# Attention over pairs of head pairs: 64x64 TensorE tiles for the last 64 keys, 32-column tiles for the denominators, and the first MLP weight tiles converted during attention and kept in DRAM

## The chip, the cores and the metric

The kernel runs on one core of a Trainium2 chip. The metric is the time of one execution in device microseconds (us); lower is better. The kernel before was timed three times: 1094.33 us is the median.

## What is computed

Three stages follow one another, all in float32 accuracy. B = 4 batches, H = 12 heads, S = 448 positions, D = 64.

```python
scores = cap * np.tanh(scale * np.matmul(q, k.transpose(0, 1, 3, 2)) / cap)
attn = np.exp(scores - np.max(scores, axis=-1, keepdims=True))
attn = attn / (np.sum(attn, axis=-1, keepdims=True) + 1e-09)
x = np.matmul(attn, v)                 # reshaped to 1792 tokens x 768
g = np.maximum(x @ w_in, 0.0) ** 2     # 768 x 2048
x = g @ w_out                          # 2048 x 768
out = ((x @ w1) * (x @ w2)) @ w3 @ w_out2
```

The weights arrive as float64 and are converted on the chip. A weight is then kept as a high and a low part (h, l) of the fast float32 format, and a product takes three matmuls: h.h, h.l, l.h.

## The kernel before

**Attention.** The 48 heads of a (batch, head) are taken as 24 pairs p. A pair has 448 keys for each of two heads, cut into four units t = 0 to 3, and the main loop counts units u = 4p + t from 0 to 95 (then 10 more steps to drain). Units 0 to 2 hold 128 keys of each of the two heads. Unit 3 holds the last 64 keys of both heads, one head in the upper, one in the lower 64 rows of the array. Scores stand keys by queries, so a unit is

- `emit_qk` (L403, two matmuls of 64 rows x 128 columns, side by side in two row halves of the array; unit 3: L405, one 128x128 matmul against a block-diagonal k that the host padded with zeros),
- `emit_tanh` and `emit_exp` on ACT (L412, L416),
- `emit_sum` on DVE (L427, for unit 3 two half-partition adds L431), which adds the exponentials up over key blocks,
- `emit_pv` (L441, two matmuls of 128 rows x 64 columns side by side in two column halves; for unit 3 the values of the other head are zeros from the host).

In the trace a matmul of q, k, v or of a sum leaves two records, a matmul of converted weights one. `emit_den` (L451) multiplies the summed exponentials with a column of ones, in two 64-column tiles; `evacuate` (L456, L460) copies results out of PSUM, and every three pairs sends the denominators through DRAM (`normalise`, L306 to L319): store, load spread over 128 partitions, reciprocal, store, load broadcast, multiply. DVE runs its instructions in the order written, so a DVE step that waits for one of these loads holds what is behind it.

**The loop** (L551 on) works on two units per even u and writes down the order of each engine: scores and tanh of u and u+1 on the even step, then products, and on the odd step pv of u-5 and u-4. Sums run four units behind.

**Side work in the loop.** `w_products` (L522 to L524) multiplies w3 with w_out2 during attention: 128 products of three matmuls of 384 columns each, in groups of 8. Their weights come in 40 pieces of 384 (or 256) columns through `w_piece` (two ACT or one POOL and one ACT instruction, five on DVE: L118, L120, L122, L136, L78). One piece may start for every 1/W_RATE = 2 units, and the w3 pieces share 7 buffers, which set how far pieces run ahead of products. `todo` at L564 spreads the products up to step W_END.

**The turn to the MLP.** When the last product is issued (step u = 88), the pool of side work is closed. Then four weight tiles of the first MLP (two of w_in, two of w_out, each in two halves) are fetched and converted by `weight_half` (8 halves on ACT and DVE), `split_x` splits the attention results of batches 0 and 1 into high and low parts, and `front(0)` (18 matmuls for each of two tiles) is issued in `ps_w`. After that the MLP loop takes `front(1)`, `back(0)` (36 matmuls), `front(2)`, `back(1)` and so on (L325 to L327); `front(2)` needs batch 2 split, `front(3)` batch 3. From there on TensorE has work to the end.

```python
W_RATE = 0.5
W_EVEN, W_END = 20, 82
...
todo = -(-products_left // max((W_END - u) // 2, 1)) if u > W_EVEN else 4
...
if w_open and u > 1 and wnext < len(wsrc) and wnext < u * W_RATE and w_may_start(wnext):
```

Of the kernel before, what the change touches and what calls it, by code (L numbers as in the profile page):

```python
# [21 lines left out]
def tile_kernel(ctx, tc, q, k, v, cap, w_in, w_out, w1, w2, w3t, wo2, out):  # L22
# [22 lines left out]
    KC = k.shape[3]  # L45
# [8 lines left out]
    GN = NP // 2  # L54
    W_RATE = 0.5
    ON_POOL = 12
    CHAINS = 2
    LAG = 2
    W_EVEN, W_END = 20, 82
# [14 lines left out]
    wp_d = dram.tile([NM, 128, DM], F32, name="wp_d")  # L74
    wc_d = dram.tile([NM, 9, 128, 2, HW], F32R, name="wc_d")
# [18 lines left out]
    def temp(dtype, pool=None):  # L94
        if pool is None:
            return cv.tile([128, S], dtype, name="cvx", bufs=6)[:, :HW]
        return pool.tile([128, HW], dtype, name="cvx", bufs=9)

    def to_f32(raw, first=ACT, pool=None, t=None):
# [8 lines left out]
        r, a = temp(I32, pool)[:, :n], temp(F32, pool)[:, :n]  # L108
# [47 lines left out]

    half_tiles = {}

    def weight_half(i, z):

        x = block()
        g = narrow(raws.pop(0), x[:, 0, :], x[:, 1, :])
        next(g)
        fetch_next()
        for _ in range(3):
            yield
            next(g, None)
        half_tiles.setdefault(i, []).append(x)
        if z == 1:
            wts[i] = [w for x in half_tiles.pop(i) for w in columns(x)]  # L170
# [98 lines left out]
    for i in range(2 * FC):  # L269
        pieces += [stream[i][:, z * HW:(z + 1) * HW] for z in range(2)]  # L270
# [29 lines left out]
    def normalise(b, n0, lag, lag2):  # L300


        rows = slice(2 * n0, 2 * (n0 + GN))
        F = 2 * GN * S // 128
        dt_ = stat.tile([128, F], F32, name="dt")
        POOL.dma_start(out=dt_, in_=den_d[b][rows].rearrange("h s -> (h s)").rearrange("(p f) -> p f", p=128))  # L306
        for _ in range(lag):
            yield
# [3 lines left out]
        for n in range(n0, n0 + GN):  # L312
            r = cv.tile([128, 2, HW], F32R, name="bs", bufs=2).bitcast(F32).rearrange("p t n -> p (t n)")[:, :S]
            for j in range(2):
                POOL.dma_start(out=r[j * D:(j + 1) * D], in_=rec_d[b][2 * n + j].partition_broadcast(D))
            for _ in range(lag2):
                yield
            a = acc[b][:, n, :]
            DVE.tensor_tensor(out=a, in0=a, in1=r, op=ALU.mult)  # L319
            normal.add((b, n))  # L320

# [40 lines left out]


    with ExitStack() as actx:
# [9 lines left out]
        NU = NPAIR * 4  # L374
        loaded, vals, units, pvs, sums, dens = {}, {}, {}, {}, {}, {}


        sel = stat.tile([128, D + GN - 1], F32, name="sel")

        def load_qk(p):  # L380
            if p < NPAIR:
                b, hp = divmod(p, NP)
                rk = ap_.tile([128, KC], F32, name="rk", bufs=2)
# [5 lines left out]
        def load_v(p):  # L389
            b, hp = divmod(p, NP)  # L390
            vals[p] = ap_.tile([128, NT, D], F32, name="rv", bufs=3)
            SP.dma_start(out=vals[p], in_=v[b, hp])

        def emit_qk(u):

            p, t = divmod(u, 4)
            rk, rq = loaded[p]
            sc = ps_s.tile([128, 2, 512], F32, name="sc")
            ks = slice(128 * t, 128 * t + 128)
            if t < 3:  # L400
                for j in range(2):
                    r = slice(j * D, (j + 1) * D)
                    PE.matmul(sc[:, j, :S], rk[r, ks], rq[r, :], start=True, stop=True, tile_position=(j * D, 0))  # L403
# [3 lines left out]
            units[u] = sc[:, :2 if t < 3 else 1, :S]  # L407

        def emit_tanh(u):
            sc = units[u]  # L410
            pt = ap_.tile([128, 2, S], F32, name="pt", bufs=7)[:, :sc.shape[1], :]
            ACT.activation(pt, sc, AF.Tanh, scale=scl)  # L412
            units[u] = pt
# [4 lines left out]
        def emit_sum(u):  # L418

            p, t = divmod(u, 4)  # L420
            if t == 0:
                return
            if t == 1:
                sums[p] = ap_.tile([128, 2, S], F32, name="sum")
            ps, x = sums[p], units[u]
            if t < 3:
                DVE.tensor_tensor(out=ps, in0=units[u - 1] if t == 1 else ps, in1=x, op=ALU.add)  # L427
            else:
                for j in range(2):
                    r = slice(j * D, (j + 1) * D)  # L430
                    DVE.tensor_tensor(out=ps[r, j, :], in0=ps[r, j, :], in1=x[r, 0, :], op=ALU.add)  # L431

        def emit_pv(u):

            p, t = divmod(u, 4)
            x = units[u]
            if t == 0:
                pvs[p] = ps_v.tile([128, 512], F32, name="pv")[:, :S]
            for j in range(2):
                w, y = (vals[p][:, 3 * j + t, :], x[:, j, :]) if t < 3 else (vals[p][:, 6 + j, :], x[:, 0, :])  # L440
                PE.matmul(pvs[p][j * D:(j + 1) * D], w, y, start=t == 0, stop=t == 3, tile_position=(0, j * D))  # L441

        def emit_den(p):

            b, hp = divmod(p, NP)
            c = hp % GN
            if c == 0:
                dens[b] = ps_d.tile([128, 512], F32, name="den")[:, :S]
            ps = sums.pop(p)
            for j in range(2):  # L450
                PE.matmul(dens[b][j * D:(j + 1) * D], sel[:, GN - 1 - c:GN - 1 - c + D], ps[:, j, :],  # L451
                          start=c == 0, stop=c == GN - 1, tile_position=(0, j * D))

        def evacuate(p):
            b, hp = divmod(p, NP)
            DVE.tensor_copy(acc[b][:, hp, :], pvs.pop(p))  # L456
            if hp % GN == GN - 1:
                n0 = hp + 1 - GN
                stg = ap_.tile([128, S], F32, name="stg", bufs=1)
                DVE.tensor_copy(stg, dens.pop(b))  # L460
                for j in range(2):
                    POOL.dma_start(out=den_d[b].rearrange("(n j) s -> n j s", j=2)[n0:n0 + GN, j, :],
# [430 lines left out]
```

## Time and profile before

| | |
|---|---|
| median of 3 runs | 1094.33 us (1094.32 to 1095.29) |
| the profiled execution | 1092.96 us, its span 1091.2 us |
| TensorE (PE) busy | 1061.9 us (97%) |
| VectorE (DVE) busy | 787.7 us (72%) |
| ScalarE (ACT) busy | 535.3 us (49%) |
| GpSimd (POOL) busy | 183.4 us (17%) |
| HBM traffic | 159 GB/s over the span |

The profile is one execution. Busy times are shares of the span; a matmul's end is modelled, so a busy TensorE can still be one that changes tiles or waits a little. The chain of waits is followed back from the last instruction. Attention takes about the first quarter of the span; the two MLPs take the rest.

### The profile page before, as it was taken

To read this page: it belongs to the slowest core of one execution; us is meant where nothing else is said; L and a number is where in the kernel's file an instruction comes from. 1 tells how busy PE (TensorE), PEld (TensorE's weight loads), DVE (VectorE), ACT (ScalarE), POOL (GpSimd) and SP (SyncE) were. 2 spreads that over 40 slices of the span, in tenths; PEclk is the share of its full clock that TensorE was granted. 3 is DMA by queue.
4 is the path that set the end of the run, shared out by engine and by line. 5 is a ranking of instruction groups with operands and counts; after the bars stand their busy time and mean duration, and the time that the engine had idled before them with its cause. 6 is when DMAs were issued, how large, how long until landed. Compare 5 with 4: busy or idle time off the path is not lost.

```text
span 1091.2 us, 14399 instructions
## 1 busy us (share of the span) xinstructions
PE 1061.9 (97%) x5088; PEld 859.8 (79%) x5088; DVE 787.7 (72%) x1494; ACT 535.3 (49%) x959; POOL 183.4 (17%) x328
## 2 busy tenths in 40 slices
PE   7999999999789999999999999999999999999998
PEld 2333557654479999999999999999989997999997
DVE  5988886556766688888888888658476679456666
ACT  7888875658667655556665555443210122210100
POOL 3221121111210011100111111002232131232110
PEclk9999999999999999999999999999999999999999
DMA  6666654325324556556565565205556466756443
GB/s 204 184 183 180 172 166 130 118 88 159 94 75 145 154 169 202 179 174 187 169 200 167 157 197 190 78 10 147 172 174 203 144 189 222 211 165 211 145 145 116
DMA packets 71383, 173.95 MB, mean 159 GB/s; under 512 B 9313, under 2 KB 18577, under 8 KB 71313
## 3 DMA queue, kind: packets, MB, share of 16 engines
q0 software_dynamic: 35456, 93.86, 27.3%
q1 hardware_dynamic: 35856, 79.18, 24.9%
q8 instruction: 40, 0.66, 0.3%
q14 instruction: 31, 0.25, 0.1%
HBM read 135.88 MB, written 37.13 MB: 159 GB/s over the span
## 4 chain that ended last, share of the span: by engine, by line
PE 82%; DVE 9%; ACT 3%; DMA 2%; issue 2%; POOL 0%; SPq 0%; DVEq 0%; POOLq 0%; ACTq 0%
PE h L326 13%; PE h L327 13%; PE h L325 13%; PE y L325 10%; PE y L326 10%; PE y L327 10%; PE pv L441 3%; PE sc L403 3%; PE h L522 2%; PE h L524 2%; PE h L523 2%; DVE sum L427 1%; PE sc L405 1%; DVE acc L764 1%; ACT pt L412 1%
## 5 line engine op out<-in xcount | busy, mean ns | idle before, releaser
L326 PE MATMUL y<-gl,wb 128*128 128x448 f32 x384 | 140.6, 366 | 1.4 <-DVE gl L78 1.4
L325 PE MATMUL y<-gh,wb 128*128 128x448 f32 x384 | 140.6, 366 | 0.0
L327 PE MATMUL y<-gh,wb 128*128 128x448 f32 x384 | 140.5, 366 | 0.0
L721 DVE TENSOR_TENSOR bt<-h,bt 128x448 f32<-128x448 f32 x96 | 59.7, 622 | 91.9 <-PE h L327 75.5
L726 ACT ACTIVATE gh<-bt 128x448 fp32r<-128x448 f32 x32 | 18.5, 579 | 205.5 <-DVE bt L724 205.5
L635 DVE TENSOR_TENSOR acc<-y,acc 128x448 f32<-128x448 f32 x168 | 98.9, 619 | 21.8 <-PE y L327 21.3
L412 ACT ACTIVATE pt<-sc,scl 128x896 f32<-128x896 f32 x96 | 84.0, 910 | 36.4 <-PE sc L403 18.9
L241 POOL DMA_DIRECT2D wc_d<-bs x72 | 38.6, 536 | 344.2 <-DVE cvx L118 150.2
L764 DVE TENSOR_TENSOR acc<-y,acc 128x448 f32<-128x448 f32 x168 | 94.1, 614 | 0.0
L416 ACT ACTIVATE pt<-pt,capt 128x896 f32<-128x896 f32 x96 | 89.9, 944 | 0.0
L441 PE MATMUL pv<-pt,rv 128*64 128x448 f32 x384 | 83.5, 556 | 2.7 <-DVE acc L456 2.7
L403 PE MATMUL sc<-rq,rk 64*128 64x448 f32 x288 | 70.6, 593 | 9.8 <-ACT pt L412 5.6
L696 POOL DMA_DIRECT2D wb<-wc_d x112 | 59.4, 544 | 113.9 <-PE h L327 91.0
L326 PEld LDWEIGHTS y<-gl,wb 128*128 128x128 f32 x384 | 72.2, 188 | 7.5 <-DVE gl L78 1.8
L325 PEld LDWEIGHTS y<-gh,wb 128*128 128x128 f32 x384 | 72.2, 188 | 6.0
L327 PEld LDWEIGHTS y<-gh,wb 128*128 128x128 f32 x384 | 72.2, 188 | 6.0
L326 PE MATMUL h<-x2l,wb 128*128 128x448 f32 x192 | 71.3, 371 | 3.1 <-DVE x2l L78 3.1
L325 PE MATMUL y<-gh,raw 128*128 128x448 f32 x192 | 71.6, 373 | 2.7 <-ACT x0h L681 0.8
L114 ACT ACTIVATE cvx<-raw 128x384 int32<-128x384 uint32 (+1 forms) x136 | 72.9, 536 | 0.0
L78 DVE TENSOR_TENSOR gl<-gr,gh 128x448 fp32r<-128x448 f32 x64 | 39.6, 619 | 44.4 <-ACT gh L358 44.4
L325 PE MATMUL h<-x0h,wb 128*128 128x448 f32 x192 | 70.5, 367 | 0.8 <-ACT gr L356 0.8
L327 PE MATMUL h<-x2h,wb 128*128 128x448 f32 x192 | 71.0, 370 | 0.0
(136 smaller groups left out, 2519.7 us busy)
## 6 DMA issues: line engine op xcount, KB each, us to landing
wb<-wc_d POOLq DMA_DIRECT2D x112, 384.0 KB, 5.9
wc_d<-bs POOLq DMA_DIRECT2D x72, 384.0 KB, 3.0
raw<-w_in SPq DMA_DIRECT2D x32, 384.0 KB, 4.0
raw<-w_out SPq DMA_DIRECT2D x32, 384.0 KB, 3.7
raw<-w SPq DMA_DIRECT2D x32, 384.0 KB, 3.6
raw<-wc_d POOLq DMA_DIRECT2D x32, 384.0 KB, 3.4
rk<-k SPq DMA_DIRECT2D x24, 256.0 KB, 3.4
raw<-w3t SPq DMA_DIRECT2D x16, 384.0 KB, 4.2
```

The lines of the kernel that those rows point to most:

```text
L114: ACT.activation(r, words[:, :, 0], AF.Copy, scale=2.0 ** -29)
L325: PE.matmul(ps, wh, xh[:, i, :], start=start and i == 0, stop=False)
L326: PE.matmul(ps, wh, xl[:, i, :], start=False, stop=False)
L327: PE.matmul(ps, wl, xh[:, i, :], start=False, stop=(i == n - 1))
L403: PE.matmul(sc[:, j, :S], rk[r, ks], rq[r, :], start=True, stop=True, tile_position=(j * D, 0))
L412: ACT.activation(pt, sc, AF.Tanh, scale=scl)
L416: ACT.activation(units[u], units[u], AF.Exp, scale=capt)
L441: PE.matmul(pvs[p][j * D:(j + 1) * D], w, y, start=t == 0, stop=t == 3, tile_position=(0, j * D))
L635: DVE.tensor_tensor(out=a, in0=y, in1=a, op=ALU.add)
L696: POOL.dma_start(out=x, in_=wc_d[s % NM, j])
L721: DVE.tensor_tensor(out=t, in0=ps[j], in1=u, op=ALU.add)
L764: DVE.tensor_tensor(out=a, in0=y, in1=a, op=ALU.add)
```

## The change

**Pairs of pairs.** Two head pairs (four heads) now make seven units of full size in place of eight: three units of the first pair, one unit with the last 64 keys of all four heads, three units of the second pair. `what(u)` gives pair and t. There are 84 units. The four-head unit takes four matmuls in 64x64 tiles for the scores (L440) and four for pv (L487), one in each quarter of the array, on diagonal places, so that the two tiles of one pair write one PSUM bank in different partitions. The zero padding of k and v is gone from the host. Sums stay as many as before: two of the four half-partition adds wait for the second pair's t = 1.

**Denominators.** `emit_den` takes two pairs at once, in four 32-column tiles (L506); groups are two pairs of pairs, then one. `normalise` waits more steps (`lags`) and loads two broadcasts ahead.

**First MLP tiles.** The eight halves of the first four tiles join the side work's list `wsrc` (now 48 pieces), one behind each w3 block, in the same 7 buffers; each is stored to `w0_d` in DRAM (two DMAs), and when the side work closes eight DMAs on POOL's queue load them back. `w_piece` may start 0.57 per unit up to u = 40 and one per unit after that. `front(0)` and now also `back(0)` come from `first_unit`, in `ps_w`; `fill` is first called when batch 0 is split. `w_store` copies a product group out of PSUM on the odd step.

```diff
+    GD = 2
+    W_RATE = 0.57, 1.0
+    W_FAST = 40
-    W_EVEN, W_END = 20, 82
+    W_EVEN, W_END = 18, 72
...
+            if kind == "w0":
+                for s, x in enumerate(parts):
+                    POOL.dma_start(out=w0_d[i, z, :, s, :], in_=x)
+                w3_done.add(wsrc[n])
...
+        def what(u):
+
+            d, x = divmod(u, 7)
+            return 2 * d + (x > LAST), x if x <= LAST else x - LAST - 1
...
-                PE.matmul(sc[:, 0, :S], rk[:, ks], rq, start=True, stop=True)
+                for z in range(2):
+                    rk, rq = loaded[p + z]
+                    for j in range(2):
+                        r, c = slice(j * D, (j + 1) * D), j ^ z
+                        PE.matmul(sc[c * D:(c + 1) * D, z, :S], rk[r, 128 * t:], rq[r, :], start=True, stop=True,
+                                  tile_position=(j * D, c * D))
...
+                pv_tile(p + 1)
+                for z in range(2):
+                    for j in range(2):
+                        r = slice((j ^ z) * D, (1 + (j ^ z)) * D)
+                        PE.matmul(pvs[p + z][j * D:(j + 1) * D], vals[p + z][r, 6, :], x[r, z, :],
+                                  start=z == 1, stop=z == 0, tile_position=((j ^ z) * D, j * D))
...
+            for z in range(2):
+                ps = sums.pop(p + z)
+                for j in range(2):
+                    r = 32 * (2 * z + j)
+                    PE.matmul(dens[b][r:r + 32], sel[:, GD - 1 - c:GD - 1 - c + 32], ps[:, j, :],
+                              start=c == 0, stop=c == n - 1, tile_position=(0, r))
...
+                lags = (6, 4, 3) if b < B - 1 else (6, 3, 1) if n == GD else (4, 3, 1)
...
-                            ready = [weight_half(i, z) for i in range(2 * FC) for z in range(2)]
-                            side.append(chain(*(split_x(b) for b in range(EARLY))))
+                            for i in range(2 * FC):
+                                halves = [block() for _ in range(2)]
+                                for z, x in enumerate(halves):
+                                    POOL.dma_start(out=x, in_=w0_d[i, z])
+                                wts[i] = [w for x in halves for w in columns(x)]
+                            side.append(splits())
```

**Order on TensorE, early in the attention, before** (sc are scores, h products, pv, den denominators; x4 counts matmuls):

```order
L403 MATMUL sc<-rq,rk 128x448 x4
L522 MATMUL h<-wb,w3h 128x384
L523 MATMUL h<-wb,w3h 128x384
L524 MATMUL h<-wb,w3l 128x384
L441 MATMUL pv<-pt,rv 64x448 x4
L403 MATMUL sc<-rq,rk 128x448 x2
L405 MATMUL sc<-rq,rk 128x448
L522 MATMUL h<-wo_388,w3h 128x384
L523 MATMUL h<-wo_388,w3h 128x384
L524 MATMUL h<-wo_388,w3l 128x384
L441 MATMUL pv<-pt,rv 64x448 x4
L451 MATMUL den<-sum,sel 64x448 x2
```

and with the change (L431 scores of full units, L440 and L487 the four-head unit, L480 pv, L506 denominators):

```order
L506 MATMUL den<-sum,sel 32x448 x4
L431 MATMUL sc<-rq,rk 128x448 x4
L589 MATMUL h<-wb,w3h 128x384
L590 MATMUL h<-wb,w3h 128x384
L591 MATMUL h<-wb,w3l 128x384
L480 MATMUL pv<-pt,rv 64x448 x2
L487 MATMUL pv<-pt,rv 64x448 x4
L431 MATMUL sc<-rq,rk 128x448 x4
L589 MATMUL h<-wo_750,w3h 128x384
L590 MATMUL h<-wo_750,w3h 128x384
L591 MATMUL h<-wo_750,w3l 128x384
L480 MATMUL pv<-pt,rv 64x448 x4
```

The rounds of scores, products and pv stay as they are; a round in seven units each has four matmuls more in its scores, its pv and its denominators, in tiles of another shape, and there are 42 rounds in place of 48.

**Order on TensorE behind the last product, before**: the products end when six units have no scores yet.

```order
L524 MATMUL h<-wo_847,w3l 128x384
L441 MATMUL pv<-pt,rv 64x448 x4
L403 MATMUL sc<-rq,rk 128x448 x2
L405 MATMUL sc<-rq,rk 128x448
L441 MATMUL pv<-pt,rv 64x448 x4
L451 MATMUL den<-sum,sel 64x448 x2
L403 MATMUL sc<-rq,rk 128x448 x4
L441 MATMUL pv<-pt,rv 64x448 x4
L403 MATMUL sc<-rq,rk 128x448 x2
L405 MATMUL sc<-rq,rk 128x448
L441 MATMUL pv<-pt,rv 64x448 x4
L451 MATMUL den<-sum,sel 64x448 x2
```

and with the change:

```order
L591 MATMUL h<-wo_831,w3l 128x384
L480 MATMUL pv<-pt,rv 64x448 x4
L506 MATMUL den<-sum,sel 32x448 x4
L487 MATMUL pv<-pt,rv 64x448 x4
L480 MATMUL pv<-pt,rv 64x448 x6
L506 MATMUL den<-sum,sel 32x448 x2
L318 MATMUL h<-x1h,wb 128x448
L506 MATMUL den<-sum,sel 32x448 x2
L318 MATMUL h<-x0h,wb 128x448
```

All scores now stand ahead of the last product, at step u = 82 of 84; behind it there are pv of six units, two groups of denominators, and the MLP. Behind these rows 35 more matmuls of `front(0)` follow, and then those of `front(1)` and `back(0)` in turns.

**Order on DVE near the end of attention, before** (conversions L118, L120, L122 and L78 wb of the first MLP tiles between sums L427, splits x0l, and the multiply of `normalise` L319):

```order
L78 TENSOR_TENSOR wb<-cvx,wb 128x384
L78 TENSOR_TENSOR x0l<-acc_66,x0h 128x448
L118 TENSOR_SCALAR cvx<-cvx 128x384
L120 SCALAR_TENSOR_TENSOR cvx<-cvx 128x384
L122 ISA cvx<-cvx 128x768
L427 TENSOR_TENSOR sum<-pt 128x896
L78 TENSOR_TENSOR x0l<-acc_66,x0h 128x448
L118 TENSOR_SCALAR cvx<-cvx 128x384
L120 SCALAR_TENSOR_TENSOR cvx<-cvx 128x384
L122 ISA cvx<-cvx 128x768
L427 TENSOR_TENSOR sum<-sum,pt 128x896
```

and with the change (L461 and L467 sums, L511 pv and L517 denominators out of PSUM, L80 splits):

```order
L517 COPY stg<-den 128x448
L80 TENSOR_TENSOR x0l<-acc_66,x0h 128x448
L461 TENSOR_TENSOR sum<-pt 128x896
L467 TENSOR_TENSOR sum<-sum,pt 64x448 x2
L80 TENSOR_TENSOR x0l<-acc_66,x0h 128x448
L511 COPY acc_69<-pv 128x448
L461 TENSOR_TENSOR sum<-sum,pt 128x896
L80 TENSOR_TENSOR x0l<-acc_66,x0h 128x448 x2
L511 COPY acc_69<-pv 128x448
L80 TENSOR_TENSOR x0l<-acc_66,x0h 128x448 x2
L517 COPY stg<-den 128x448
```

No conversion stands there any more.

## Rows read from the trace of the kernel before

**Rows 1.** The page: span, TensorE's busy time, its granted clock in 40 slices.
```profile
span 1091.2 us, 14399 instructions
PE 1061.9 (97%) x5088; PEld 859.8 (79%) x5088; DVE 787.7 (72%) x1494; ACT 535.3 (49%) x959; POOL 183.4 (17%) x328
...
PEclk9999999999999999999999999999999999999999
```

**Rows 2.** Busy time by stretch: length; PE, PEld, DVE, ACT, POOL; clock, DMA share, GB/s.
```profile
0.00:20.07 20.07, 14.07 (x45) 4.48 (x45) 8.43 (x18) 14.02 (x18) 5.75 (x9) 1.00 0.64 204
20.07:115.45 95.38, 90.46 (x397) 35.65 (x397) 86.32 (x160) 81.48 (x115) 24.71 (x33) 0.98 0.60 178
115.45:253.22 137.77, 137.77 (x677) 83.07 (x675) 85.51 (x167) 90.85 (x132) 25.79 (x48) 1.00 0.47 144
253.22:311.50 58.28, 48.12 (x209) 29.12 (x208) 45.50 (x87) 42.99 (x81) 12.42 (x23) 0.97 0.36 105
311.50:1091.20 779.70, 771.46 (x3764) 707.51 (x3764) 561.90 (x1065) 305.98 (x616) 114.71 (x216) 1.00 0.53 163
```

**Rows 3.** The same view for line L522 alone: one matmul of each product.
```profile
20.07:115.45 95.38, 10.87 (x19) 3.69 (x19) 0.98 0.60 178
115.45:253.22 137.77, 40.72 (x109) 20.49 (x109) 1.00 0.47 144
```

**Rows 4.** The chain of waits, 109 to 118 us: start, length, what.
```profile
109.65 0.95 PE sc L403 x4
110.60 0.95 PE sc L405 x2
111.55 0.17 PE h L522
...
113.12 1.65 PE pv L441 x8
114.77 0.75 PE den L451 x4
115.53 1.71 PE sc L403 x8
117.23 0.37 PE h L522
```

**Rows 5.** The timeline at 131.55 to 131.60 us: start, length, engine, line, count.
```profile
131.52 0.20 PEld L441 LDWEIGHTS pv<-pt,rv 128*64 128x64 f32 x4 [0.25 <-issue]
131.52 0.60 PE L441 MATMUL pv<-pt,rv 128*64 128x448 f32 x2
```

**Rows 6.** Waits in the first 312 us: total, times, longest.
```profile
DVE acc L319 <- DMA bs<-rec_d: 22.4, 6, 5.1
```

**Rows 7.** TensorE's timeline: three of its idle times, with what ended them.
```profile
65.90 1.29 PE L403 MATMUL sc<-rq,rk 64*128 64x448 f32 x4 [2.10 <-ACT pt L412]
...
98.37 1.72 PE L441 MATMUL pv<-pt,rv 128*64 128x448 f32 x8 [2.19 <-DVE acc L456]
...
288.61 2.41 PE L451 MATMUL den<-sum,sel 128*64 128x448 f32 x4 [2.74 <-DVE sum L431]
```

**Rows 8.** One pair of the first stage, by the view of Rows 2.
```profile
71.74:80.67 8.93, 8.93 (x43) 3.57 (x41) 8.53 (x16) 8.26 (x13) 1.75 (x4) 1.00 0.78 222
```

**Rows 9.** The chain of waits where the MLP starts.
```profile
298.88 2.40 DMA rec_d<-dt
...
302.09 3.05 DMA bs<-rec_d
...
305.23 0.62 DVE acc L319
...
312.57 0.74 PE h L326
```

**Rows 10.** The page: POOL's issue of a weight load, and its time to landing.
```profile
L696 POOL DMA_DIRECT2D wb<-wc_d x112 | 59.4, 544 | 113.9 <-PE h L327 91.0
...
wb<-wc_d POOLq DMA_DIRECT2D x112, 384.0 KB, 5.9
```

More of the change, by code (lines that the diff above doesn't have):

```diff
@@ L298, in split_x, with normalise @@
             yield
[L300 to L305, printed above, removed]
+    def normalise(b, n0, n1, lags):
+        rows = slice(2 * n0, 2 * n1)
+        dt_ = stat.tile([128, 4 * GD * S // 128], F32, name="dt")[:, :2 * (n1 - n0) * S // 128]
         POOL.dma_start(out=dt_, in_=den_d[b][rows].rearrange("h s -> (h s)").rearrange("(p f) -> p f", p=128))
-        for _ in range(lag):
+        for _ in range(lags[0]):
             yield
@@ L361, in front, with back, first_unit @@
             yield
+    def back(n, pool, name="y", some=NO // 2):
+        c, b = divmod(n, B)
+        gh, gl = gtiles[n % 2]
+        ws = [wts[4 * c + FC + m] for m in range(FC)]
+        for o in range(NO):
+            y = pool.tile([128, 512], F32, name=name)[:, :S]
+            products(y, [w[o] for w in ws], gh, gl)
+            a = acc[b][:, o, :]
+            if c == 0:
+                ACT.activation(a, y, AF.Copy)
+            else:
+                DVE.tensor_tensor(out=a, in0=y, in1=a, op=ALU.add)
+            if c == NC - 1 or o == NO - 1:
+                flush()
+            if c == NC - 1 and (b == 0 or b == 1 and o >= NO // 2):
+                xh, xl = (x[:, o, :] for x in xs[b])
+                ACT.activation(xh, a, AF.Copy)
+                late.append((xl, a, xh))
+            tick(3)
+            if (o + 1) % some == 0:
+                yield
+    def first_unit(pool):
+        yield from front(0, pool)
+        flush()
+        yield from back(0, pool, "h", 2)
     with ExitStack() as actx:
@@ L423, in emit_sum @@
             if t == 1:
[L424 to L427, printed above, removed]
-            else:
[L429 to L441, printed above, removed]
+                sums[p] = ap_.tile([128, 2, S], F32, name="sum", bufs=3)
@@ new lines, in emit_sum, with pv_tile @@
+            if t < LAST:
+                DVE.tensor_tensor(out=sums[p], in0=units[u - 1] if t == 1 else sums[p], in1=units[u], op=ALU.add)
+            z = p % 2
+            if t == LAST or z and t == 1:
+                x = units[u - z * 2]
+                for j in range(2):
+                    r = slice((j ^ z) * D, (1 + (j ^ z)) * D)
+                    DVE.tensor_tensor(out=sums[p][r, j, :], in0=sums[p][r, j, :], in1=x[r, z, :], op=ALU.add)
+        def pv_tile(p):
+            pvs[p] = ps_v.tile([128, 512], F32, name="pv")[:, :S]
@@ L500, in w_piece @@
-            g = narrow(*blocks[0], on=DVE, first=POOL if n < ON_POOL else ACT, pool=wq)
+            kind, i, z = wsrc[n]
+            raw = wraw.pop(n)
+            if kind == "wo":
+                x = block() if i < 5 else wq.tile([128, 2, HW], F32R, name=f"wo{i}{z}")
+                parts = [x[:, 0, :], x[:, 1, :]]
+            else:
+                nj = raw.shape[-1] // 128
+                tiles = [wq.tile([128, 3, 128], F32R, name=f"w3{s}", bufs=W3)[:, :nj, :] for s in "hl"]
+                parts = [x.rearrange("p a c -> p (a c)") for x in tiles]
@@ L501, in w_piece @@
+            g = narrow(raw, *parts, on=DVE, first=POOL if n < ON_POOL else ACT, pool=wq)
             next(g)
@@ L605, in tile_kernel @@
                 advance(norms)
-            while chains or ready:
-                while ready and len(chains) < CHAINS:
-                    chains.append(ready.pop(0))
-                advance(chains)
-            while fronts < FC:
-                first = first or front(0, ps_w)
-                next(first)
-                fronts += 1
+            assert not w_open
+            while side:
+                advance(side)
+            for _ in fill:
+                pass
     mp = ctx.enter_context(tc.tile_pool(name="mlp", bufs=2, reuse_waits="tile"))
@@ L870 @@
         "q": pairs(q),
-        "k": kk,
+        "k": pairs(k),
         "v": vv,
```

257 lines of the change are left out of this document (122 added, 135 removed).

## The prediction

> **What bounds the kernel now.** I read the page first, then busy time by stretch, then the chain of waits, then single idle times. TensorE is busy for 97% of the span, at the upper level of its granted clock in every slice [rows 1]. So only what TensorE does, or waits for, can change the time. The stretches [rows 2] part the span by what ends last. From 20.07 to 115.45 us (units 8 to 47, ten head pairs) DVE is busy 86.3 of 95.4 us, and TensorE 90.5. From 115.45 to 253.22 (ten more pairs, and 109 of the 128 products [rows 3]) TensorE is busy without a gap. From 253.22 to 311.5 (last eight units, first MLP matmuls) it idles for 10.2 us, and DVE (45.5) and ACT (43.0) are busy for much of it: they convert the first MLP tiles there. From 311.5 on the MLPs run: 779.70 us for 3764 matmuls, 0.207 each. That part is not touched. I call the three stretches A, B and C.
>
> **Prices on TensorE** [rows 4]. Eight score matmul records take 1.71 us, four take 0.95. So one unit is 0.76, and 0.19 is what the first matmul behind a change of tile shape loses. A product behind the scores loses the same (0.37 against 0.17 to 0.18 for the next); three such matmuls, 0.525, make a product. pv of two units is 1.65: 2 x 0.75 and a change of 0.15. The denominators behind pv, in tiles of the same shape, are 0.75 and lose nothing. A pair is two rounds: 1.71 + 0.19 + 1.65 = 3.55, and 0.95 + 0.95 + 1.65 + 0.75 = 4.30; together 7.85. Test on B: 10 x 7.85 + 109 x 0.525 + 1.9 (the last scores and the change behind them) = 137.6, where the row has 137.8.
>
> **A pair of pairs after the change.** Seven units are 3.5 rounds of 3.55, or 12.43. The four-head unit breaks the row of equal tiles once in the scores and once in pv: 2 x 0.15. The denominators of both pairs, in four 32-column tiles, are 0.75 and a change of 0.15. Sum 13.63, against 15.70: 2.07 saved, twelve times: 24.8 us of TensorE's work. The trace has no group of four 64x64 tiles. Its bounds are 0.75 us (all four at once, as two tiles are now) and 3.0 (one after the other). I take 0.75: two tiles run together in both directions, row halves in the scores and column halves in pv, at the same price, so quarters are nearest to that. The row behind it [rows 5] shows the two first matmuls of pv running, with four weight loads at their side.
>
> A change of shape might be dear only towards full tiles: the denominators of before change nothing, so these rows do not price a change among column tiles. [...]
>
> **A.** TensorE needs 10 x 6.81 + 16 x 0.525 = 76.5 us for the same ten pairs (with the change 112 products are left at unit 42). DVE does what it did: the adds stay the same in number, and 0.57 pieces x 3.5 units are two pieces a pair, as 0.5 x 4 were. So DVE bounds A: at least its busy 86.3, at most the 95.4 of now. Among what it loses now are loads of `normalise` [rows 6], behind which TensorE idles (2.10 and 2.19 us) [rows 7]. The new lags wait six and four units where three were waited for, so the loads are there. In a pair without such a wait DVE is busy 8.53 of 8.93 us [rows 8]. I take the middle, 91: **4.4 us saved** (0 to 9).
>
> **B.** From the scores of unit 42 to the last product at unit 82 there are 40 units x 1.947 + 112 x 0.525 + 1.9 = 138.6, against 137.8, for 11.4 pairs in place of ten. The pieces of the first MLP tiles lie beside it: by the price of a pair with its two pieces [rows 8], DVE has 11.4 x 8.53 = 97 us and ACT 11.4 x 8.26 = 94 to do, under 139. But the weights come later, through the same seven buffers, so I add 1.5 us of waits (0 to 7). **2.3 us lost.**
>
> **C.** Behind the last product TensorE has no scores left: pv of six units (6 x 0.75 + 0.45), two groups of denominators (2 x 0.90), then `front(0)`, `back(0)` and `front(1)`: 108 x 0.207 = 22.4. Sum 29.1. Waits: the last denominators wait for the last sum, as at 288.61 [rows 7], 2.7; `front` reuses the one buffer of `ps_w` behind ACT, 1; splits of batch 2 stand on DVE behind multiplies of the last `normalise`, whose loads take 2.40 and 3.05 [rows 9]. There 7.3 us pass between the multiply at 305.23 and TensorE's next matmul at 312.57; I take 4 of them, since the same order remains (0 to 7.3). Sum 36.8, against 58.3: **21.5 us saved** (11 to 29). What hides the conversions now gone from C was DVE and ACT; their work moved into B, under TensorE. SP's queue fetches these eight halves earlier, in the same number. POOL gets 16 stores, 8 loads and 16 more small DMAs, at 0.54 us of issue [rows 10]: 22 us, spread over stretches where it is busy 63 of 291 us [rows 2]. The eight loads issue in 4.4 us; the first lands after 5.9 [rows 10], before TensorE has done pv and denominators (6.8 + 2.7).
>
> **Sum.** -4.4 + 2.3 - 21.5 = -23.6 us, against the profiled execution of 1092.96: 1069.4. The median of the runs lies 1.4 above it: 1094.33 - 23.6, about **1071 us**. About 0.2% (2 us) is what a measurement of this kernel tells from no change.
>
> **Rivals.**
>
> 1. *Two at a time.* The four 64x64 tiles run as two and two, 1.5 us a group: 1.5 us more per pair of pairs. A hides it (76.5 + 7.5 = 84, under 91); B holds 5.7 pairs of pairs, 8.6 us; C one pv group, 0.75. Sum 9.3: **1080 us**. Against it speaks the timeline [rows 5], where the column halves share all rows and still load weights while matmuls run; for it: no row has four. [...]
>
> 2. *One at a time: slower than before.* If tiles on the four quarters wait for each other, a group takes 3.0 us, 4.5 more per pair of pairs. In A TensorE then needs 76.5 + 22.5 = 99, 8 over DVE's 91; B grows by 25.7, C by 2.3. Sum 36: **1107 us**. It turns the sign from about 2.4 us a group on, where A's slack is used up as well. Against it: the two shapes that the chain shows [rows 4] both run two at a time.
>
> 3. *Late weights.* The stored tiles come back over the same engines as SP's next fetches. C moved 105 GB/s [rows 2], and 384 KB at that rate is 3.7 us; then the fourth half lands 17 us behind the last product, where `front(0)` asks for it at about 15. The waits in B may also be the full 7. Either gives 5 to 8 us: **1077 us**.
>
> **How the numbers follow.** Forecast 0.70, rival 1 0.11, rival 3 0.12, rival 2 0.05, and 0.02 that gains and new waits cancel. The low end takes A at -9, B at +0.8 and C at -25: 1061. The high end takes rival 1 together with half of rival 3's waits: 1087. Faster by over 0.2%: 0.93; within: 0.02; slower: 0.05.
>
> **What would show it.** In the changed profile: L440 with its eight records at 0.9 us in the chain, not 1.65; L506 at 0.9 or less; DVE nearly without idle time up to unit 42, at about 111 us; no gap on TensorE from there to the last product at about 250; from there some 37 us to the first matmul on batch 2. It is wrong if the four-head records start in pairs 0.75 us apart (rival 1), if TensorE idles before L589 for weights of a product, or if it idles before L318 for the stored tiles (rival 3).

## The result, and the profile after

The changed kernel takes **1077.28 us** (median of 4 runs, 1076.24 to 1079.31), the kernel before beside it 1094.32: a ratio of 0.9846, 95% interval [0.9829, 0.9863]. So it is faster by 17.0 us, where the prediction had 23.3. The forecast of 1071 lies 6.3 us below the measured time, and the range of 1061 to 1087 holds it. The profiled execution of the change took 1076.87 us, 16.09 less than that of the kernel before.

The page of the changed kernel, as in [rows 1]:

```profile
span 1075.1 us, 14546 instructions
...
PE 1047.7 (97%) x5136; PEld 846.2 (79%) x5136; DVE 790.0 (73%) x1502; ACT 527.8 (49%) x927; POOL 204.6 (19%) x368
...
PEclk9899999999899999999999999999999999999999
```

TensorE is busy 14.2 us less, and at 97% of the span still what bounds the kernel. Its granted clock, 9 in every slice before (a 9 stands for 0.90 or more; by stretch it was 0.97 to 1.00 [rows 2], and 0.50 from 66.52 to 69.93, from 288.38 to 291.80 and from 312.28 to 315.69 us), now shows an 8 in two, at 27 to 54 and at 269 to 296 us.

Busy time by stretch (columns as in [rows 2]), cut where the work is the same as before: start of unit 8, scores of unit 42, end of the last product, first matmul on batch 2, first matmul on batch 3, end.

```profile
0.00:21.18 21.18, 14.40 (x57) 4.40 (x57) 8.64 (x18) 14.76 (x18) 6.68 (x9) 1.00 0.67 212
21.18:108.17 86.99, 80.50 (x396) 28.52 (x396) 83.03 (x157) 78.64 (x104) 23.58 (x32) 0.94 0.63 187
108.17:246.50 138.33, 138.08 (x756) 81.13 (x752) 112.40 (x221) 106.00 (x148) 41.05 (x76) 1.00 0.60 181
246.50:279.73 33.23, 29.72 (x147) 20.71 (x147) 16.74 (x31) 16.00 (x32) 16.26 (x31) 1.00 0.52 155
279.73:302.20 22.47, 19.88 (x80) 16.47 (x78) 14.87 (x30) 16.81 (x35) 2.36 (x4) 0.85 0.26 73
302.20:1075.10 772.90, 765.12 (x3709) 694.92 (x3707) 554.34 (x1049) 295.54 (x594) 114.71 (x216) 1.00 0.54 163
```

The same view of the kernel before, for the last three of these stretches:

```profile
253.22:305.76 52.54, 44.43 (x193) 26.45 (x193) 39.90 (x75) 40.65 (x76) 11.27 (x21) 0.97 0.38 110
305.76:325.63 19.87, 16.75 (x73) 14.51 (x72) 14.12 (x29) 12.90 (x27) 1.15 (x2) 0.91 0.20 58
325.63:1091.20 765.57, 758.40 (x3709) 695.68 (x3707) 553.37 (x1049) 295.43 (x594) 114.71 (x216) 1.00 0.54 165
```

Read down the lengths against each other. Unit 42 has its scores at 108.17, where unit 48 had them at 115.45: 7.3 us won (8.4 in the stretch itself, less 1.1 lost ahead of unit 8). The next stretch is 138.33 against 137.77: 0.6 lost. From the last product to batch 2, 33.23 against 52.54, and from there to batch 3, 22.47 against 19.87: 16.7 won. And then the last row, the one that the change does not touch: 772.90 against 765.57. **7.3 us lost**, with the same 3709 matmul records, the same clock of 1.00, and 6.7 of the loss are busy time of TensorE (765.12 against 758.40), not waiting. The sum, -7.3 + 0.6 - 16.7 + 7.3, is the -16.1 of the two spans.

The chain of waits in the stretch that TensorE bounds (columns as in [rows 4]):

```profile
126.30 1.65 PE pv L480 x8
127.96 0.89 PE den L506 x8
128.84 1.71 PE sc L431 x8
130.55 0.90 PE pv L480 x4
131.45 0.91 PE pv L487 x8
...
138.50 1.65 PE pv L480 x8
140.16 0.91 PE sc L440 x8
141.07 0.95 PE sc L431 x4
142.02 0.38 PE h L589
```

All eight records of a four-head group take 0.91 us, in the scores (L440) and in pv (L487), and the denominators in 32-column tiles (L506) 0.89. That is 0.75 and a change of shape of 0.15, as the sum had it. TensorE's timeline and its weight loads at one such group (columns as in [rows 5]):

```profile
161.26 0.21 PEld L440 LDWEIGHTS sc<-rq,rk 64*64 64x64 f32 x8 [0.65 <-issue]
161.27 0.98 PE L440 MATMUL sc<-rq,rk 64*64 64x448 f32 x8
```

and the same row in a narrower window, 161.2 to 161.4 us, with what had started by then:

```profile
161.27 0.61 PE L440 MATMUL sc<-rq,rk 64*64 64x448 f32 x4
```

The first four of the eight records start within 0.02 us of each other, last 0.59 us each and lie inside 0.61 us: the four tiles run side by side. All eight loads lie inside the first 0.21 us.

Where TensorE waits at the turn to the MLP (its timeline, as in [rows 7]):

```profile
253.94 0.44 PE L318 MATMUL h<-x1h,wb 128*128 128x448 f32 x1 [0.62 <-DMA wb<-w_d]
256.00 0.94 PE L506 MATMUL den<-sum,sel 128*32 128x448 f32 x4 [1.62 <-DVE sum L461]
...
285.63 0.48 PE L319 MATMUL h<-x2l,wb 128*128 128x448 f32 x1 [1.65 <-DVE x2l L80]
...
288.69 0.74 PE L319 MATMUL h<-x2l,wb 128*128 128x448 f32 x1 [0.72 <-DVE x2l L80]
289.23 0.57 PE L320 MATMUL h<-x2h,wb 128*128 128x448 f32 x1
```

The stored tiles are 0.62 us late, the last sum 1.62, low parts of batch 2 1.65 and 0.72. Matmuls behind these last two take longer: the granted clock of 288.69 to 293.50 is 0.57 (0.50 from 285.99 to 292.81), and the step from matmul to matmul at 0.50 is 0.37 us in place of 0.207 at 1.00. What DVE did ahead of them, by its timeline:

```profile
279.31 0.62 DVE L311 TENSOR_TENSOR acc<-acc,bs 128x448 f32<-128x448 f32 x1 [4.66 <-DMA bs<-rec_d]
279.85 0.62 DVE L80 TENSOR_TENSOR x2l<-acc,x2h 128x448 fp32r<-128x448 f32 x1
...
284.42 0.62 DVE L311 TENSOR_TENSOR acc<-acc,bs 128x448 f32<-128x448 f32 x1
284.96 1.15 DVE L80 TENSOR_TENSOR x2l<-acc,x2h 128x448 fp32r<-128x448 f32 x2
```

A multiply of `normalise` for batch 3 waits 4.66 us for its load, and the splits of batch 2 (L80) stand behind it and its successors, and behind conversions of the next tiles (L120 to L124, from 282.97 on).

### The profile page after: what moved, and what is told of

It is laid out like the page before. It is cut to its first block, busy times and chain, and to the rows that moved or that the text cites. A ratio compares the mean times of both kernels' runs of the same rounds, so it can differ in the third digit from the quotient of the medians.

```text
span 1075.1 us, 14546 instructions
## 1 busy us (share of the span) xinstructions
PE 1047.7 (97%) x5136; PEld 846.2 (79%) x5136; DVE 790.0 (73%) x1502; ACT 527.8 (49%) x927; POOL 204.6 (19%) x368
## 4 chain that ended last, share of the span: by engine, by line
PE 85%; DVE 11%; ACT 2%; issue 1%; DMA 1%; SPq 0%; POOL 0%; DVEq 0%; ACTq 0%
PE h L318 14%; PE h L319 14%; PE h L320 14%; PE y L318 10%; PE y L319 10%; PE y L320 10%; PE sc L431 3%; PE pv L480 3%; PE h L589 2%; DVE sum L461 2%; PE h L591 2%; PE h L590 2%; DVE sum L467 1%; DVE acc L825 1%; DVE cvt L124 1%
## 5 line engine op out<-in xcount | busy, mean ns | idle before, releaser
L318 PE MATMUL y<-gh,wb 128*128 128x448 f32 x372 | 137.0, 368 | 0.0
L319 PE MATMUL y<-gl,wb 128*128 128x448 f32 x372 | 136.9, 368 | 0.0
L320 PE MATMUL y<-gh,wb 128*128 128x448 f32 x372 | 136.1, 366 | 0.0
L787 ACT ACTIVATE gh<-bt 128x448 fp32r<-128x448 f32 x32 | 18.5, 579 | 206.7 <-DVE bt L785 206.7
L447 ACT ACTIVATE pt<-sc,scl 128x896 f32<-128x896 f32 x84 | 80.9, 1013 | 27.2 <-PE sc L431 14.4
L451 ACT ACTIVATE pt<-pt,capt 128x896 f32<-128x896 f32 x84 | 86.9, 1047 | 0.0
L431 PE MATMUL sc<-rq,rk 64*128 64x448 f32 x288 | 71.5, 608 | 12.6 <-ACT pt L447 8.4
L320 PEld LDWEIGHTS y<-gh,wb 128*128 128x128 f32 x372 | 69.9, 188 | 6.7
L318 PEld LDWEIGHTS y<-gh,wb 128*128 128x128 f32 x372 | 69.7, 187 | 7.0
L319 PEld LDWEIGHTS y<-gl,wb 128*128 128x128 f32 x372 | 69.9, 188 | 6.2
L319 PE MATMUL h<-x2l,wb 128*128 128x448 f32 x192 | 72.1, 376 | 2.6 <-DVE x2l L80 2.6
L80 DVE TENSOR_TENSOR gl<-gr,gh 128x448 fp32r<-128x448 f32 x64 | 39.6, 621 | 45.5 <-ACT gh L351 45.5
L318 PE MATMUL h<-x2h,wb 128*128 128x448 f32 x192 | 71.9, 374 | 0.0
L320 PE MATMUL h<-x2h,wb 128*128 128x448 f32 x192 | 71.8, 374 | 0.0
```

Of the source, the lines that this page charges most:

```text
L80: DVE.tensor_tensor(out=l, in0=src, in1=h.bitcast(F32), op=ALU.subtract)
L318: PE.matmul(ps, wh, xh[:, i, :], start=start and i == 0, stop=False)
L319: PE.matmul(ps, wh, xl[:, i, :], start=False, stop=False)
L320: PE.matmul(ps, wl, xh[:, i, :], start=False, stop=(i == n - 1))
L431: PE.matmul(sc[:, j, :S], rk[r, 128 * t:128 * t + 128], rq[r, :], start=True, stop=True, tile_position=(j * D, 0))
L447: ACT.activation(pt, units[u], AF.Tanh, scale=scl)
```

## Experiments

Eleven kernels were run, for three questions: what the untouched MLP stretch lost its 7.3 us to; what each part of the change is worth; and which waits are left. The expectations count time from the first matmul (3.9 to 4.2 us into the span) where they speak of the first matmul on batch 3, and end at the start of the last matmul: the 302.20 and 772.90 of the rows above are 298.3 and 767.1 there.

### What the MLP stretch lost

The changed kernel needs fewer small tiles (`sel` is 132 bytes per partition in place of 264, `dt` 112 in place of 84), and so everything allocated behind them lies 96 bytes lower (96 and not 104, which fits tiles rounded up to 32 bytes): the ring of weights `wb` begins at byte 91392 of a partition in place of 91488, and `raw`, x2, x3, gh1 and gl1 move by the same 96. x0, x1 and gh0 come from the other side and stay. The first runs moved them with unused bytes and changed no instruction.

The changed kernel, 32 bytes:

```diff
     capt = stat.tile([128, 1], F32, name="capt")
+    stat.tile([128, 8], F32, name="pad")
```

> The changed kernel with 32 unused bytes per partition ahead of the tiles of weights, so that raw, wb, x2, x3, gh1 and gl1 begin 32 bytes past a multiple of 64, as they did in the kernel before (in the changed kernel they begin on a multiple of 64); no instruction differs. In the traces at hand the same MLP work, from the first matmul on batch 3 to the end, takes 760.7 us before and 767.1 after, at a granted clock of 1.00 in both, by a median step from matmul to matmul of 203 and 206 ns. Theory 1, the place of the tiles sets the step: 203 ns here, and about 6 us less: 1071. Theory 2, the step differs by execution or by chip: no difference by this edit, 1077, and the step may be either. Theory 3, the changed order of work or its traffic costs the 6 us: 206 ns and 1077.

Measured: 1071.70 us, ratio 0.9798 [0.9781, 0.9815]. The time is what theory 1 named, 5.6 us less than the change, but the median step stayed at 206; a part of the steps became much shorter (those on the low parts of batches 0 and 1 take 199.7 and 199.4 ns in the mean, 206.3 and 206.6 in the change; by up to 0.2 ns such means hang on where the stretch is taken to begin).

The kernel before, the same line:

> The kernel before with the same 32 unused bytes, which puts raw, wb, x2, x3, gh1 and gl1 on multiples of 64; no instruction differs. Theory 1 (place of the tiles): the step becomes 206 ns, and the time about 6 us longer, 1100. Theories 2 and 3 (execution, or changed order): 1094, and by theory 3 a step of 203 ns.

Measured: 1094.88 us, ratio 1.0009 [1.0000, 1.0018]; the median step 204. So theory 1 in its first form, that a multiple of 64 makes the step 206, is wrong: this kernel has all those tiles on multiples of 64 and loses 0.9 us, not 6. What the address does is finer than that. The next run put every tile of the changed kernel where the kernel before had it: `stat.tile([128, 24], F32, name="pad")`.

> The changed kernel with 96 unused bytes per partition, which puts raw, wb, x2, x3, gh1 and gl1 exactly where the kernel before had them; x0 and x1 lie there in both already. The first four runs: from the first matmul on batch 3 to the end 767.1 us with the ring of weights wb at 91392 (the change), 766.3 at 91392 (late tiles), 762.7 at 91424, 762.0 and 761.5 at 91520 (two different kernels, with the same histogram of steps), 760.7 at 91488 (the kernel before). Theory 1, refined: the addresses as such set the step. Then 760.7 here, a median step of 203, and 1077.3 less 6.4: 1071, or a little under the run with 32 bytes. Rival: what 32 bytes gave was the move off a multiple of 64 or 128, and this gives the 762.7 of that run: 1072 to 1073. Rival: the changed work has its own price in the MLP stretch, which no address takes away: above 763.

Measured: **1071.10 us**, ratio 0.9794 [0.9780, 0.9809]. By stretch, up to the first matmul on batch 3 and from there:

```profile
0.00:302.19 302.19, 277.57 (x1428) 148.51 (x1429) 235.66 (x454) 232.25 (x333) 90.83 (x152) 0.99 0.58 174
302.19:1068.50 766.31, 758.57 (x3709) 695.00 (x3707) 553.60 (x1049) 296.02 (x594) 114.76 (x216) 1.00 0.54 165
```

The first row ends where the change's does (302.20), the second has TensorE's busy time of the kernel before: 758.57 against 758.40, for 3709 records in both. So 6.6 of the 7.3 us (772.90 to 766.31) are the place of the tiles; the 0.7 left is no more than runs of one kernel differ by. The same number from all runs, sorted by the place of the ring:

| `wb` at | x0 and x1 | kernels | TensorE busy, first matmul on batch 3 to the end (us) |
|---|---|---|---|
| 91392 | as in the change | the change; late tiles; splits first; old lags | 765.12; 764.34; 764.93; 764.98 |
| 91392 | 32 bytes lower | 32 bytes ahead of gh0 | 762.63 |
| 91392 | as in the change; x2, x3 as in the kernel before | 96 bytes in the last pool | 761.41 |
| 91424 | as in the change | 32 bytes | 760.61 |
| 91520 | as in the change | before with 32 bytes; 64-column denominators | 759.70; 759.53 |
| 91488 | as in the change | before; 96 bytes; both gains | 758.40; 758.57; 758.26 |
| 91488 | 32 bytes lower | both gains and 32 bytes | 758.81 |

Kernels that differ in their attention but have equal addresses agree within 0.8 us; the changed kernel at other addresses differs from itself by up to 6.6. Two runs asked whose address it is. The first moved x0 and x1 alone:

```diff
+                            xp.tile([128, 8], F32, name="xpad")
                             new_gtiles(xp)
```

> The changed kernel with 32 unused bytes in the pool of batches 0 and 1 alone: x0 and x1 move down by 32 bytes, everything else stays (wb at 91392, x2 and x3 too). In the trace of the change a matmul on x2 or x3 takes 206.7 ns to the next, on x0 high 203.4, on x0 low 206.3. Theory 1 (addresses): the steps on x0 and x1 change by some ns, those on x2 and x3 stay at 206 to 207; the time moves by what x0 and x1 move, within 4 us to either side of 1077. Rival (one property of the whole run, as a clock or a chip): all steps move together or none does.

Measured: 1074.09 us, ratio 0.9822 [0.9808, 0.9837]. The mean step on the low parts of x0 and x1 fell from 206.3 and 206.6 to 202.8 and 199.3 ns, those on x2 and x3 stayed at 206.4 to 206.6: theory 1 as expected. The second moved x2, x3, gh1 and gl1 alone, with `mp.tile([128, 24], F32, name="pad", bufs=1)` ahead of them:

> The changed kernel with 96 unused bytes in the last pool alone: x2, x3, gh1 and gl1 lie where the kernel before had them, the ring of weights wb, raw and the rest stay where the change put them (wb at 91392). Steps in the change: 206.6 to 206.7 ns on x2 and x3, and TensorE is busy for 765.1 us in the 3709 matmuls from the first on batch 3 to the end; at the addresses before: 203.6 to 204.2 and 758.4 to 758.6. Theory a, the address of the streamed tile sets its step: x2 and x3 fall to about 204, and the busy time by some 1000 matmuls times 2.6 ns and a share for gh1 and gl1: 761 to 763, 1073 to 1075. Theory b, the address of the weights sets it: 206 to 207 stays on x2 and x3, 765 and 1077. Theory c, their places against each other: some third value on x2 and x3, with x0 and x1 as in the change.

Measured: 1073.91 us, ratio 0.9812 [0.9795, 0.9829]. The steps on x2 and x3 became 204.9 to 205.5, neither the 206.7 of the change nor the 204 of the kernel before: theory c's third value. But the steps on the low parts of x0 and x1, which did not move, fell too, from 206.3 and 206.6 to 203.9 and 203.5. No theory had that. So the step of a matmul follows neither from the address of what it streams nor from that of its weights alone, nor, here, from the two against each other. That the place of the tiles sets it is shown; by what mechanism stays open. A rival that no run tests is that what other engines write at the same time counts: gh1 and gl1, which moved here, are written by ACT and DVE while TensorE works on other batches (in the change 14 writes each to tiles gh and gl from 302 to 400 us, of about 0.58 and 0.62 us).

### What the parts of the change are worth

Attention alone: the first four tiles are converted at the end, as before (`weight_half` put back, the eight `w0` entries taken out of the list of pieces).

```diff
-        wsrc += first
...
+                            ready = [weight_half(i, z) for i in range(2 * FC) for z in range(2)]
...
+                while ready and len(chains) < 2:
+                    chains.append(ready.pop(0))
```

> The changed attention alone: the first four MLP tiles are fetched and converted where the kernel before did it, at the end of attention, two at a time, and not stored; the rest is the changed kernel. By the prediction's terms the eight conversions lie in the third stretch again, where DVE and ACT are what ends last: 8 halves of about 2.4 us on DVE, so 12 to 20 us longer: 1089 to 1097. Rival: the attention's own shortening is what saved the third stretch, and the conversions hide beside pv and denominators: 1077 to 1081.

Measured: 1092.93 us, ratio 0.9996 [0.9983, 1.0008]. The stretches from the last product to batch 2, to batch 3 and to the end:

```profile
234.10:297.50 63.40, 48.26 (x211) 27.33 (x210) 42.09 (x78) 38.85 (x69) 14.69 (x28) 0.87 0.36 109
297.50:318.87 21.37, 17.94 (x73) 15.04 (x73) 13.98 (x28) 16.21 (x34) 1.15 (x2) 0.84 0.24 66
318.87:1090.60 771.73, 764.34 (x3709) 694.40 (x3707) 554.53 (x1049) 295.79 (x594) 114.67 (x216) 1.00 0.54 163
```

The products end 12.4 us earlier than in the change, since no tiles are converted beside them, and from there to batch 3 it takes 84.8 us in place of 55.7. So moving the conversions gains 29.1 there for 12.4 beside the products: it is worth 16.7 us. What is left, 325.63 to 318.87, is 6.8 us for the pairs of pairs, and the place of the tiles (764.34) eats it. The first theory holds. The granted clock is lower in the first of these rows as well, 0.87 where the change has 1.00, so the 16.7 holds matmuls at the lower clock besides waits.

Denominators in 64-column tiles, pair by pair:

```diff
-                    r = 32 * (2 * z + j)
-                    PE.matmul(dens[b][r:r + 32], sel[:, GD - 1 - c:GD - 1 - c + 32], ps[:, j, :],
+                    r, k = j * D, 2 * c + z
+                    PE.matmul(dens[b][r:r + D], sel[:, 3 - k:3 - k + D], ps[:, j, :],
```

> The changed kernel with denominators in tiles of 64 columns, two tiles at a time, pair by pair (rows packed by the same sums, group sizes kept). Four matmuls then take two groups of 0.75 us without a change of shape, where the trace after shows 0.89 for all eight records, change included: 0.6 us more per pair of pairs. In the stretch that TensorE bounds (from unit 42 to the last product, 5.7 pairs of pairs) that is 3.4 us, 0.6 to 1.2 in the tail, nothing earlier: 1081. [...]

Measured: 1073.73 us, ratio 0.9817 [0.9800, 0.9834]: less than the change, which the expectation misses. The chain, and the MLP stretch:

```profile
152.20 1.66 PE pv L480 x8
153.86 1.50 PE den L506 x8
```

```profile
304.82:1073.30 768.48, 759.53 (x3709) 694.83 (x3707) 553.99 (x1049) 296.05 (x594) 114.67 (x216) 1.00 0.54 164
```

The denominators take 1.50 where the change takes 0.89. From the scores of unit 42 to the last product that makes

```profile
107.41:249.37 141.96, 141.00 (x754) 82.71 (x753) 113.54 (x222) 106.87 (x149) 36.81 (x69) 1.00 0.59 178
```

141.96 us in place of 138.33: **3.6 us lost** for 3.4 expected. Unit 42 came 0.8 earlier in this run, and the tail cost nothing more (0.6 to 1.2 was expected), so batch 3 starts 2.6 later, at 304.82 in place of 302.20. But its larger `sel` moved the ring to 91520, and the MLP stretch gave back 5.6 us of TensorE's time (765.12 to 759.53). Read by the total alone, this run would have said that 32-column tiles cost time. They save 3.6 us.

`normalise` with its old lags:

```diff
-                lags = (6, 4, 3) if b < B - 1 else (6, 3, 1) if n == GD else (4, 3, 1)
+                lags = (3, 3, 3) if b < B - 1 else (6, 3, 1) if n == GD else (4, 3, 1)
```

> The changed kernel with normalise waiting three units for each of its loads in batches 0 to 2, as before, in place of six, four and three. The prediction held that the longer waits take DVE's idle time for these loads away and that this is most of what the first stretch (units 8 to 42) gains. Then DVE waits again at L294 and L311, 1 to 2 us a group in the first stretch, where DVE ends last: 1078 to 1082, with the first scores of unit 42 at 110 to 112 in place of 108.2. Rival: the loads land within three units of the shorter rounds as well, or TensorE's shorter work is what the stretch gains: 1077 and 108 to 109.

Measured: 1083.33 us, ratio 0.9904 [0.9888, 0.9921], and the scores of unit 42 at 112.72, 4.5 us later. DVE's waits in that stretch, and idle times of ACT and TensorE behind them:

```profile
DVE acc L311 <- DMA bs<-rec_d: 3.0, 1, 3.0
```

```profile
83.94 1.01 ACT L447 ACTIVATE pt<-sc,scl 128x896 f32<-128x896 f32 x1 [4.88 <-DVE sum L461]
...
85.00 1.86 PE L431 MATMUL sc<-rq,rk 64*128 64x448 f32 x4 [4.59 <-ACT pt L447]
```

In the changed kernel no wait of DVE is listed from 21 to 108 us. One wait of 3.0 us, ended at 77.56, is enough to cost 4.5: behind it the sums are late, the tanh of the next unit waits for a tile that such a sum sets free, and the scores wait for the tanh, so that TensorE idles for 4.59. The theory holds, at a price somewhat over its range. The mark itself moves by 2 us: the other runs with the new lags have the scores of unit 42 at 106.30 to 108.44, all well ahead of 112.72.

### The waits that are left

Two waits in the first stretch were taken away by no run. TensorE waits for a tanh, and ACT for a sum on DVE, as in the run before, though DVE itself waits for nothing:

```profile
46.60 1.01 ACT L447 ACTIVATE pt<-sc,scl 128x896 f32<-128x896 f32 x1 [4.66 <-DVE sum L467]
47.66 1.86 PE L431 MATMUL sc<-rq,rk 64*128 64x448 f32 x4 [3.22 <-ACT pt L447]
...
100.50 1.91 ACT L447 ACTIVATE pt<-sc,scl 128x896 f32<-128x896 f32 x2 [1.55 <-DVE sum L467]
101.56 3.29 PE L431 MATMUL sc<-rq,rk 64*128 64x448 f32 x8 [2.45 <-ACT pt L447]
```

The granted clock behind them is 0.50 (47.66 to 53.90) and 0.62 (101.56 to 106.00). In the run with 96 unused bytes ahead of the weights (the one of 1071.10 us) the same two waits stand, 3.17 and 2.48 us, but the clock of the stretch is 1.00, and it takes 85.49 us in place of 86.99:

```profile
21.50:106.99 85.49, 76.55 (x397) 26.98 (x397) 81.48 (x154) 77.08 (x101) 23.77 (x31) 1.00 0.62 185
```

Batch 2 split ahead of the multiplies of `normalise` and of the conversions:

```diff
+                for _ in range(4 if n == 1 else 0):
+                    next(xsplit, None)
                 if n > 0:
                     advance(norms)
-                for _ in range(2):
+                for _ in range(0 if n == 1 else 2):
                     next(xsplit, None)
```

> The changed kernel, where DVE and ACT split batch 2 ahead of the last multiplies of normalise and of the conversions of the next tiles (four steps a quarter in place of two, before the multiplies); addresses as in the change. In the trace of the change TensorE waits 1.65 and 0.72 us for low parts of batch 2 behind those multiplies, and then runs 16 matmuls at 0.374 in place of 0.207, 2.7 us. Theory (the prediction's fourth wait in the third stretch: batch 2 stands on DVE behind normalise): both waits and most of the slow matmuls go, 3 to 5 us less: 1072 to 1074. Rival: the wait moves on to batch 3, whose multiplies come later now, or to ACT, which makes the high parts: 1076 to 1078.

Measured: **1071.86 us**, ratio 0.9801 [0.9786, 0.9816], at the addresses of the change. From the first matmul on batch 2 to that on batch 3:

```profile
279.99:297.36 17.37, 16.72 (x79) 14.41 (x78) 12.99 (x26) 14.33 (x32) 2.07 (x4) 1.00 0.35 106
```

17.37 us in place of 22.47, and the granted clock 1.00 in place of 0.85. The two waits were 2.4 us; the other 2.7 are the slow matmuls behind them, which went with them. Nothing of it was given back at batch 3.

Both gains together:

> The changed kernel with both edits that gained alone: batch 2 split first (first matmul on batch 3 at 293.4 us in place of 298.3) and 96 unused bytes (760.6 us from there to the end in place of 767.1). They touch different stretches, so the gains add: 1077.3 less 4.9 and 6.5, 1066; first matmul on batch 3 at 293 to 294, and 760.6 from there. Rival: the faster matmuls of the MLP stretch meet a later wait (ACT or DVE behind the earlier splits) and give 1 to 3 us back: 1067 to 1069.

Measured: **1066.40 us**, ratio 0.9738 [0.9725, 0.9751], 0.7 us short of the sum of the two. Batch 3 starts at 298.57 (294.5 by the count of the expectation, just outside its 293 to 294), 1.2 us later than with the first edit alone, and TensorE is busy for 758.26 us from there. With x0 and x1 lowered besides:

> The same with x0 and x1 32 bytes lower besides, which took 2.0 to 7 ns from the steps on their low parts with the ring at 91392 (206.3 to 202.8, 206.6 to 199.3). If each operand's own address sets the step, x0 and x1 fall again by as much, some 750 matmuls by 1 to 2 ns in the mean: 1 us less than the run with both edits, 1065. If what counts is an address beside the ring's, the effect at this place of the ring is another, and may be a loss: 1064 to 1068, with the steps on x2 and x3 unchanged at 203.7 to 204.2 either way.

Measured: 1065.63 us, ratio 0.9737 [0.9724, 0.9750], no difference from the run before. The steps on the low parts of x0 and x1 became 205.0 (from 204.7 and 203.7), and those on x2 and x3, which had not moved, 202.5 to 203.3 (from 203.6 to 204.0). The expectation that these stay was wrong, as in the run on the last pool. There is a pattern, though: the steps on x0 to x3 are now, within 0.5 ns, those of the two kernels with the ring at 91520 (x0 high 205.3 against 205.4 in both, x2 high 202.9 against 202.8 and 202.9). Against those, the ring and x0 to x3 all lie 32 bytes lower here, so their distances from each other are the same. The second pair of runs with equal distances, the ring at 91424 and x0 and x1 lowered with the ring at 91392, agrees within 0.4 ns on x1, x2 and x3, but not on x0 (high 203.3 and 201.8, low 199.7 and 203.0). So distances between tiles seem to count for more than addresses, but do not settle it.

## Why the prediction was right, and where it was not

**TensorE's prices: right.** Four 64x64 tiles at 0.75 and a change at 0.15 came out as 0.91, the denominators as 0.89 for 0.90 expected. Rivals 1 and 2 fall with the first of these rows: of the four tiles two share each row half, and four matmuls and all eight loads lie inside 0.61 us. 64-column denominators behind pv, in tiles of the same shape, lose nothing (1.50 for two groups of 0.75), where a change of shape costs about 0.15 (0.91 and 0.89 less 0.75). What the 0.15 us are, no run shows.

**Stretch A: right in kind, too small.** Forecast 4.4, measured 7.3, within the 0 to 9 given; the 1.1 us lost ahead of unit 8 are not in the sum. DVE bounds it, busy 83.03 of 86.99 us (under the 86.3 taken as the floor), and the longer lags are most of the gain: without them 4.5 of the 7.3 are gone. TensorE needs what the sum gave it: 76.55 us where the clock stayed at 1.00, for 76.5. With 4.0 us more of busy time at the lower clock (0.94 over the stretch), 80.50, the stretch grew by 1.5 only.

**Stretch B: right.** Forecast 138.6 without waits, measured 138.33; the 1.5 us that were added for late weights did not come.

**Stretch C: right in kind, too large.** Forecast 21.5; to the first matmul on batch 3, 16.7. Moving the conversions is worth as much, 16.7 us by its own run, as argued. The largest error in the sum is that its two sides end at different work. The 58.3 runs to 311.50, where the kernel before was 16 matmuls into batch 2; the 36.8 has the 108 matmuls ahead of batch 2 and no more. These 16, 3.3 us, stand on neither side of the forecast. The reading of [rows 9] is wrong with it: 312.57 is the next matmul of the chain, not of TensorE, which had been on batch 2 since 305.76 and had waited twice:

```profile
305.76 0.36 PE L325 MATMUL h<-x2h,wb 128*128 128x448 f32 x1
...
308.97 0.47 PE L326 MATMUL h<-x2l,wb 128*128 128x448 f32 x1 [1.00 <-DVE x2l L78]
...
312.57 0.74 PE L326 MATMUL h<-x2l,wb 128*128 128x448 f32 x1 [2.12 <-DVE x2l L78]
```

To the first matmul on batch 2, where the prediction looked for some 37 us, the change takes 33.23: the 29.1 of work and the 3.7 of the first two waits make 32.8, and the 4 us for the splits come behind that matmul. Left out besides are the matmuls at a granted clock of about 0.50 behind two short waits, 2.7 us, and the higher price of the first matmul behind a wait or behind a turn from `front` to `back` (about 0.30 in place of 0.207, ten times: 1.0). The waits themselves, 6.1 us by the timeline, are under the 7.7 of the sum.

**The step that failed is "That part is not touched".** No instruction of the MLP is, but most of its tiles were moved by 96 bytes, and TensorE lost 6.7 us of busy time there. With the tiles put back, the changed kernel takes 1071.10, the forecast. That is luck in part: A and B together gave 4.6 more than forecast, C 4.8 less, and so up to batch 3 the forecast of 23.6 met 23.4.

**Rival 3 has the right time for the wrong reason.** Late weights would have given 1077; the stored tiles cost 0.62 us.

## What to carry to other kernels

Split a measured time at marks where the work on both sides is the same, and look at the stretch that should be equal first: here it hid 7 us, as much as a part of the change was worth, and in one experiment it turned the sign of what was being tested. A change in the size of small tiles moved the tiles allocated behind them by 96 bytes here, so hold the addresses with unused bytes before two variants are compared. Where a step that waits for a load holds what stands behind it, as DVE's multiply here with its wait of 4.66 us, put what TensorE waits for ahead of it: it was worth 5 us here, over half of it in matmuls at a granted clock of about 0.50 behind waits of 1.65 and 0.72 us.

## What the runs showed of the hardware that was not expected

The step between equal matmuls (128x128 weights, 448 columns, granted clock 1.00) was between 199.3 and 206.7 ns in the mean, by where tiles lie in SBUF: 758.3 to 765.1 us for 3709 of them. It is the same, within 0.8 us of that sum, in every kernel with the same addresses, and it isn't a matter of a multiple of 64: of four places of the ring 91392 is the slowest, and 91520, on a multiple of 64 too, among the faster ones. Tiles that didn't move changed their step when others did (203.9 from 206.3, 202.8 from 204.0), which no theory here explains; in one pair of runs, where the ring and x0 to x3 moved together by 32 bytes, the steps on x0 to x3 stayed within 0.5 ns.

The same wait did not always cost the same. Behind an idle time of TensorE of 2.45 us at 101.56 the scores of two units took 3.29 us in the change; behind one of 2.48 at 101.88 they took 1.92 in the run with 96 unused bytes. The granted clock fell in the one execution (0.62 from 101.56 to 106.00) and not in the other (1.00 from 21.50 to 106.99). No run shows why.
